# A gated linear attention and its feed-forward layer in one kernel: keys and queries turned in token pairs, and a new order of steps behind the 60th

## The chip, the cores and the metric

The kernel runs on one core of a Trainium2 chip. A core has five engines that run side by side and keep their own order: TensorE (matmuls; in the profile PE, its weight loads PEld), VectorE (DVE), ScalarE (ACT), GpSimd (POOL) and SyncE (SP, which here issues every DMA). They meet through semaphores alone. The metric is the time of one execution in microseconds of device time.

## The reference

For each of 4 batches and 8 heads, over 768 tokens with 48 channels, a state of 48 x 48 decays channel by channel and takes in one token's key and value; each token's query reads it. The result, 3072 tokens by 384, goes through two matmuls (384 x 2048 and 2048 x 384) with a gate between them.

```python
for t in range(S):
    state = alpha[:, :, t, :, None] * state + np.einsum('bhd,bhe->bhde', k[:, :, t], v[:, :, t])
    y[:, :, t] = np.einsum('bhd,bhde->bhe', q[:, :, t], state)
...
h = x @ w_in
relu6 = np.clip(h + 3.0, 0.0, 6.0)
g = h * relu6 / 6.0
return (g @ w_out).astype(np.float32)
```

## The kernel before

**Attention.** The 3072 tokens are 24 chunks of 128 (6 to a batch, `j` from 0 to 23); a chunk holds its 8 heads as 4 pairs (`NP`), each pair in 128 rows (two heads of 48 channels, padded to 64), with 128 tokens along the free dimension. So alpha, keys and queries have to be turned from token rows to channel rows. For chunks below `FIRST` = 6 TensorE does it (`transposed`, steps `ta`, `tk`, `tq`, L282) from the `rings` tiles into PSUM. From chunk 6 on the DMAs of `load_akq` lay 32-token blocks out in `quads` (two per name, `j % 2`), and a DVE transpose of 32 x 32 blocks (`by_blocks`, L286) finishes it: its source has four blocks `v` side by side, token number is 4u + v, and so it writes every fourth float of the target, 16 bytes apart.

With alpha turned in the tile `aX` (129 columns a pair, the first always 0; step `ca`), two DVE scans run over it: `decay` (step `r`, L309) backwards, giving R, products of alpha from a token to the chunk's end, and its reciprocal at the first column into `ini`; `growth` (step `p`, L320) forwards, giving P, growing products that start from that reciprocal. `scaled` (steps `k` and `q`, L332) multiplies keys by R and queries by P. TensorE then makes the scores of two half chunks (`sc`, L346), DVE masks them (`m`, L356), ScalarE lays the queries beside them (`qa`, L366), and `attend` (`ya`, `yb`, L456) multiplies scores and queries with values and state. For the state the keys go back to token rows: `kb` on TensorE below chunk 8, from there on by a DVE transpose (`kt`, L391), a write to DRAM (`kw`, L396) and a read back (`kr`, L404). `update` (`u`, L430) multiplies keys and values, `next_state` (`sm`, L440) adds on DVE, `decayed_state` (`st`, L409) multiplies on POOL, `place_state` (`sv`, L419) copies on ScalarE. The scores, updates and attends are matmuls of 64 rows or 32 to 64 columns; every other matmul of the kernel fills 128 x 128.

**Feed-forward.** Two chunks make a group `g` (0 to 11). `keep_x` (`cy`) puts a chunk's result in the group's `xT`. Groups 0 and 1 use plain matmuls (`fa`, `fb`, `f`: L490, L479); group 0 also the plain second matmul (`b`, L517). From group 2 on the first matmul is done by 20 products of sums of blocks (`M`, L603), for which DVE makes sums of x (`xc`, L540 to L544); ScalarE keeps partial products (`n`, L609), DVE makes outputs of them (`o`), ScalarE and DVE gate them (`e`, L495, and `h`, L499). From group 1 on the second matmul is done by 7 products of half blocks (`P`, L706) with sums on DVE (`s`, L650 and L667), and `K`, `G`, `O` keep, add and store them. The weights come in 16 slices as 64-bit floats (`w`, L162 and L166) and are rounded to 32 bits by ScalarE, DVE and POOL (`d1` to `d4`, L186 to L217).

**Order.** Nothing is scheduled by a planner at build time: the string given to `run` at the end of the kernel lists 1798 steps, name and indices joined by dots (`M.5.14` is product 14 of group 5; `sc.13.3.2` is the scores of chunk 13 in PSUM banks 3 and 2), and each engine, SyncE with its DMAs too, gets its instructions in that order. `z` is a matmul that keeps TensorE running in the first 25 us.

Of the kernel before, what the change touches and what calls it, by code (L numbers as in the profile page):

```python
# [17 lines left out]
def kernel(  # L18
# [208 lines left out]
    Ps = consts.tile([C, NP * W], FP, tag="P", name="P")  # L227
# [46 lines left out]
    def transposed(name, j, i=None):  # L274
        if j >= FIRST:
            t = (K_t if name == "k" else Q_t)[j] = (Ks if name == "k" else Qs)[j % 2]
            by_blocks(t, name, j)
            return
        t = bank("t" + name, j, i)
        src = ring[name, j % NR]  # L280
        for p in range(NP):
            nc.tensor.transpose(  # L282
                t[:, p], src[:, 2 * p : 2 * p + 2].rearrange("s h d -> s (h d)"), ident)

    def by_blocks(to, name, j):
        nc.vector.transpose(out=to.rearrange("r p (u v) -> r p v u", v=V),  # L286
                            in_=quads[name, j % NQ][:, :, :, 0:BLK])

# [15 lines left out]
    def decay(j):  # L304

        n = NP * W
        ax, ic = aX[j % 2], ini[j % 2]
# [5 lines left out]
        nc.vector.reciprocal(out=ic.rearrange("r (p w) -> r p w", w=W)[:, :, 0:1],  # L313
                             in_=R_t[j][:, :, 0:1])

    def growth(j):

        n = NP * W
        P_t[j] = Ps
        nc.vector.tensor_tensor_scan(  # L320
            out=P_t[j], data0=aX[j % 2][:, 0:n], data1=ini[j % 2], initial=0.0,
            op0=ALU.mult, op1=ALU.add)

    def scaled(name, j):

        if j < FIRST:
# [5 lines left out]
        nc.vector.tensor_tensor(out=t, in0=src, in1=by, op=ALU.mult)  # L332
# [424 lines left out]
    with tc.manual_schedule():  # L757
# [15 lines left out]
               q.4 st.4 d1.9 fr.1.1.0 fg.1.1 sv.4.0 f.1.0.2 ca.5 sc.4.1.0 u.4.1.0 fg.0.6 r.5 d1.4
               f.1.7.0 r.6 f.1.3.3 d4.8 d2.4 w.10 tk.5.3 d4.9 w.11 dx.4 fr.1.7.1 sm.4.0 d3.4 w.12
               d2.10 qa.4.0 fg.1.7 fr.1.3.1 m.4 lq.5 d1.10 f.1.6.0 d3.10 d1.12 d4.4 fr.1.0.0 f.1.2.1
               p.5 fg.1.3 d2.12 k.5 fg.1.0 d3.12 d4.10 fr.1.6.1 sm.4.1 tq.5.1 sv.4.1 lk.6 w.13
               fr.1.2.0 d1.11 f.1.4.2 d2.11 d4.12 fg.1.6 q.5 d3.11 p.6 d2.13 la.7 fr.1.4.1 fg.1.4
               f.1.5.0 lv.5.0 qa.4.1 fg.1.2 kb.5.3 fr.1.5.1 w.15 d4.11 d2.15 ca.7 ya.4.1 qa.5.1 tk.6
# [162 lines left out]
```

## Time and profile before

| what | before |
|---|---|
| median of 3 runs | 533.5 us (532.84 to 533.6) |
| the profiled execution's own time | 533.63 us |
| its span, first to last instruction | 531.8 us |
| TensorE matmuls busy | 524.3 us, 99%, clock 1.00 throughout |
| VectorE busy | 475.6 us, 89% |
| ScalarE busy | 261.4 us, 49% |
| DMA, share of 16 engines' span | 42.2% |

The profile is of one execution. A matmul's duration covers its way through the array, so that consecutive ones overlap; the distance from start to start, or from the start of a row of equal matmuls to the next row's start, tells the pace. A group's line gives line number, engine, operation, tiles and shapes, how many, busy time in us, mean ns of one, and the idle time of the engine just before them with what ended it. Line numbers are those of the kernel before.

### The profile page before, as it was taken

How to read it: one execution, taken by the hardware profiler on the slowest of the kernel's cores; microseconds unless marked ns; L12 is line 12 of the kernel's file. 1: busy time of each engine (PE TensorE's matmuls, PEld its weight loads, DVE VectorE, ACT ScalarE, POOL GpSimd, SP SyncE). 2: the span in 40 equal slices, each digit the busy share in tenths (PEclk: the TensorE clock that was granted, in tenths of full speed). 3: DMA queues.
4: the chain of work that ended last, by engine and by line, in shares of the span. 5: the costliest groups of instructions: out<-in, count | busy, mean ns of one | idle time of the engine just before them, and what ended most of it. 6: DMA issues, size and time to landing. Idle time of an engine off the chain costs nothing.

```text
span 531.8 us, 15076 instructions
## 1 busy us (share of the span) xinstructions
PE 524.3 (99%) x6290; PEld 494.0 (93%) x6290; DVE 475.6 (89%) x839; ACT 261.4 (49%) x513; POOL 50.3 (9%) x71
## 2 busy tenths in 40 slices
PE   8999999999999999999999999999999999999997
PEld 5798886789999999999999999999999999999997
DVE  7999999999999999999999999998999999486471
ACT  4888875212664453542673554544454454443330
POOL 5333353100000100000000000000000000000000
PEclk9999999999999999999999999999999999999999
DMA  9999867005363253453463553443531532010000
GB/s 177 246 241 251 247 153 177 2 2 133 74 150 84 64 118 77 115 123 89 95 156 85 120 136 91 96 107 69 145 78 20 129 98 48 1 33 7 9 17 30
DMA packets 124100, 54.40 MB, mean 102 GB/s; under 512 B 83328, under 2 KB 116864, under 8 KB 124032
## 3 DMA queue, kind: packets, MB, share of 16 engines
q1 hardware_dynamic: 124032, 53.44, 42.2%
q8 instruction: 49, 0.80, 0.7%
q14 instruction: 19, 0.16, 0.1%
HBM read 44.50 MB, written 8.91 MB: 100 GB/s over the span
## 4 chain that ended last, share of the span: by engine, by line
PE 85%; DVE 7%; ACT 4%; DMA 1%; issue 1%; SPq 1%; POOL 0%; DVEq 0%; ACTq 0%
PE m_ps L706 36%; PE m_ps L603 31%; PE m_ps L479 4%; PE m_ps L517 4%; PE t_ps L456 4%; PE t_ps L346 2%; PE t_ps L430 2%; DMA rings<-in_q_dram 1%; DVE A L356 1%; ACT A L366 1%; DVE g_sb L540 1%; ACT r L495 1%; ACT raw L186 1%; DVE g_sb L499 1%; SPq L251 1%
## 5 line engine op out<-in xcount | busy, mean ns | idle before, releaser
L706 PE MATMUL m_ps<-w,g_sb 128*128 128x192 f32 x704 | 121.7, 326 | 0.0
L609 ACT COPY g_sb<-m_ps 128x512 f32<-128x512 f32 x110 | 63.5, 584 | 104.2 <-PE m_ps L603 86.4
L706 PEld LDWEIGHTS m_ps<-w,g_sb 128*128 128x128 f32 x704 | 113.7, 190 | 0.6 <-DVE g_sb L667 0.3
L706 PE MATMUL m_ps<-rings,g_sb 128*128 128x192 f32 x528 | 91.7, 327 | 0.2 <-DVE g_sb L650 0.2
L706 PEld LDWEIGHTS m_ps<-rings,g_sb 128*128 128x128 f32 x528 | 85.3, 190 | 0.6 <-DVE g_sb L650 0.5
L603 PE MATMUL m_ps<-xc,w 128*128 128x128 f32 x640 | 83.5, 277 | 0.0
L603 PEld LDWEIGHTS m_ps<-xc,w 128*128 128x128 f32 x640 | 77.9, 192 | 1.1
L495 ACT ACTIVATE r<-g_sb,half 128x512 f32<-128x512 f32 x80 | 57.0, 722 | 29.8 <-DVE g_sb L499 11.9
L499 DVE SCALAR_TENSOR_TENSOR g_sb<-r,g_sb 128x512 f32<-128x512 f32 x80 | 53.5, 682 | 8.7 <-ACT r L495 8.4
L603 PE MATMUL m_ps<-xT,raw 128*128 128x128 f32 x400 | 52.8, 277 | 0.0
L603 PEld LDWEIGHTS m_ps<-xT,raw 128*128 128x128 f32 x400 | 48.8, 192 | 0.5 <-ACT g_sb L609 0.2
L409 POOL TENSOR_TENSOR st<-sm,R 128x192 f32<-128x192 f32 x20 | 12.6, 630 | 358.2 <-DVE sm L440 300.5
L650 DVE TENSOR_TENSOR g_sb<-g_sb 128x512 f32<-128x512 f32 (+1 forms) x55 | 42.1, 792 | 3.7 <-PE m_ps L706 3.5
L603 PE MATMUL m_ps<-xT,w 128*128 128x128 f32 x320 | 42.0, 277 | 0.0
L603 PEld LDWEIGHTS m_ps<-xT,w 128*128 128x128 f32 x320 | 39.0, 192 | 0.4
L366 ACT COPY A<-q 48x256 f32<-48x256 f32 x88 | 35.4, 403 | 7.3 <-DVE q L332 6.1
L356 DVE TENSOR_TENSOR A<-t_ps,mask 64x256 f32<-64x256 f32 x96 | 36.2, 416 | 1.2 <-PE t_ps L346 0.8
L479 PE MATMUL m_ps<-xT,w 128*128 128x256 f32 x144 | 33.3, 384 | 0.5 <-POOL w L217 0.3
L603 PE MATMUL m_ps<-xc,raw 128*128 128x128 f32 x240 | 32.1, 277 | 0.1
L479 PEld LDWEIGHTS m_ps<-xT,w 128*128 128x128 f32 x144 | 26.5, 190 | 5.3 <-POOL w L217 0.9
L540 DVE TENSOR_TENSOR g_sb<-g_sb 128x512 f32<-128x512 f32 x40 | 27.2, 682 | 4.6 <-ACT g_sb L609 4.6
L309 DVE TENSOR_TENSOR_SCAN R<-t,ones 128x516 f32<-128x516 f32 x24 | 29.6, 1233 | 1.6 <-ACT t L300 1.6
(105 smaller groups left out, 726.9 us busy)
## 6 DMA issues: line engine op xcount, KB each, us to landing
raw<-in_moe_w_out_dram SPq DMA_DIRECT2D x8, 768.0 KB, 5.5
raw<-in_moe_w_in_dram SPq DMA_DIRECT2D x6, 768.0 KB, 7.3
v<-in_v_dram SPq DMA_DIRECT2D x48, 96.0 KB, 3.1
out_dram<-oh SPq DMA_DIRECT2D x44, 96.0 KB, 1.8
far<-kq SPq DMA_DIRECT2D x64, 64.0 KB, 2.2
kb<-far SPq DMA_DIRECT2D x64, 64.0 KB, 2.0
aq<-in_alpha_dram SPq DMA_DIRECT2D x36, 96.0 KB, 2.5
kq<-in_k_dram SPq DMA_DIRECT2D x36, 96.0 KB, 2.5
```

The source lines that it names most:

```text
L309: nc.vector.tensor_tensor_scan(out=reverse(R, n - 1, n), data0=reverse(ax, n, n), data1=reverse(ones, n, n), initial=0.0, op0=ALU.mult, op ...
L356: nc.vector.tensor_tensor(out=to[:, a], in0=sc[a][half], in1=mask[half, half].unsqueeze(1).to_broadcast([HB, NP, HB]), op=ALU.mult)
L366: nc.scalar.copy(out=to[:, a], in_=Q_t[j][64 * a : 64 * a + D, :, half])
L456: nc.tensor.matmul(y_of(j, (i + 1) // 2, p)[:, HB * b : HB * b + HB], vb[:, p, e : e + 32], A_t[j][:, b, 2 * p + a], start=(b == 0 and i = ...
L479: nc.tensor.matmul(h[:, f], w1[:, kk, o : o + C], xT_t[g][:, kk], start=(kk == 0), stop=(kk == KT - 1))
L495: nc.scalar.activation(out=to, in_=h, func=AF.Relu, bias=half, scale=1.0 / 6.0)
L499: nc.vector.scalar_tensor_tensor(out=to, in0=r, scalar=1.0, in1=h, op0=ALU.min, op1=ALU.mult)
L540: eng.tensor_tensor(out=out, in0=in0, in1=in1, op=ALU.add if s1 > 0 else ALU.subtract)
L603: nc.tensor.matmul(acc[g][i][:, f * C : (f + 1) * C], spots[w][:, f * C : (f + 1) * C], x_of(g, x), start=(first and f == 0), stop=last, s ...
L609: nc.scalar.copy(out=slots[z], in_=acc[g][i])
L650: nc.vector.tensor_tensor(out=out, in0=in0, in1=in1, op=ALU.subtract)
L706: nc.tensor.matmul(to[g], a, rhs[:, f], start=(first and f == 0), stop=(last and f == HF - 1), skip_group_check=True)
```

## The change

Keys and queries of chunks 6 to 23 are turned by `turned` (L291 of the new kernel) instead of `by_blocks`: the target is a new tile per name (`kt`, `qt`) with the four blocks `v` split in two pairs (w, b), so that tokens 4u + 2w and 4u + 2w + 1 stand next to each other and the next write is 8 bytes on. `scaled` reads pairs from that tile in token order (`in_pairs`) and writes the dense K and Q tiles, which the transposes filled before. P no longer has a tile: below chunk 6 it stands in `qt`, from there on it is scanned over alpha's own tile `aX`, whose first columns a memset on POOL clears again after the queries are scaled. `ini` is one tile instead of two.

The first 60 steps of the order are the same. All steps behind them stand in another order, and PSUM banks are assigned anew; how often each step occurs is unchanged. In the extract of the diff the order is cut to the first lines behind the 60th step and to the places round `M.5.14` (both orders), `u.12`, `lk.17` and `la.18` (the new one).

```diff
@@ -102,14 +102,13 @@
 
 
 
-    aX, ini = [], []
+    aX = []
     for r in range(2):
         t = consts.tile([C, NP * W + 1], FP, tag=f"ax{r}")
         nc.vector.memset(t, 0.0)
         aX.append(t)
-        t = consts.tile([C, NP * W], FP, tag=f"ini{r}")
-        nc.vector.memset(t, 0.0)
-        ini.append(t)
+    ini = consts.tile([C, NP * W], FP, tag="ini")
+    nc.vector.memset(ini, 0.0)
     ones = consts.tile([C, NP * W + 1], FP, tag="ones")
     nc.vector.memset(ones, 0.0)
     nc.vector.memset(ones[:, 1:].rearrange("r (p w) -> r p w", w=W)[:, :, W - 1 : W], 1.0)
@@ -224,7 +223,10 @@
     Rs, Qs, Ks, kbs = (
         [consts.tile([C, *shape], FP, tag=f"{name}{r}", name=f"{name}{r}") for r in range(2)]
         for name, shape in (("R", (NP * W,)), ("q", (NP, C)), ("k", (NP, C)), ("kb", (NP, C))))
-    Ps = consts.tile([C, NP * W], FP, tag="P", name="P")
+    places = {name: consts.tile([C, NP * W], FP, tag=f"{name}t", name=f"{name}t")
+              for name in "kq"}
+    turns = {name: t[:, 0 : NP * C].rearrange("r (w p n) -> r w p n", w=2, p=NP)
+             for name, t in places.items()}
 
     def bank(name, j, i):
         ps_t[name, j] = banks[i].rearrange("r (p n) -> r p n", p=NP)
@@ -273,8 +275,7 @@
 
     def transposed(name, j, i=None):
         if j >= FIRST:
-            t = (K_t if name == "k" else Q_t)[j] = (Ks if name == "k" else Qs)[j % 2]
-            by_blocks(t, name, j)
+            turned(name, name, j)
             return
         t = bank("t" + name, j, i)
         src = ring[name, j % NR]
@@ -286,6 +287,17 @@
         nc.vector.transpose(out=to.rearrange("r p (u v) -> r p v u", v=V),
                             in_=quads[name, j % NQ][:, :, :, 0:BLK])
 
+    def turned(to, name, j):
+        nc.vector.transpose(
+            out=turns[to].rearrange("r w p (u b) -> r p w b u", b=V // 2),
+            in_=quads[name, j % NQ].rearrange("r p (w b) d -> r p w b d", w=2)[..., 0:BLK])
+
+    def in_pairs(to):
+        return turns[to].rearrange("r w p (u b) -> r p u w b", b=V // 2)
+
+    def pairs(x):
+        return x.rearrange("r p (u w b) -> r p u w b", w=2, b=V // 2)
+
     def reverse(t, first, n):
 
         one = t[:, first : first + 1]
@@ -304,33 +316,35 @@
     def decay(j):
 
         n = NP * W
-        ax, ic = aX[j % 2], ini[j % 2]
+        ax = aX[j % 2]
         R = Rs[j % 2]
         nc.vector.tensor_tensor_scan(
             out=reverse(R, n - 1, n), data0=reverse(ax, n, n), data1=reverse(ones, n, n),
             initial=0.0, op0=ALU.mult, op1=ALU.add)
         R_t[j] = R.rearrange("r (p w) -> r p w", w=W)
-        nc.vector.reciprocal(out=ic.rearrange("r (p w) -> r p w", w=W)[:, :, 0:1],
+        nc.vector.reciprocal(out=ini.rearrange("r (p w) -> r p w", w=W)[:, :, 0:1],
                              in_=R_t[j][:, :, 0:1])
 
     def growth(j):
 
         n = NP * W
-        P_t[j] = Ps
-        nc.vector.tensor_tensor_scan(
-            out=P_t[j], data0=aX[j % 2][:, 0:n], data1=ini[j % 2], initial=0.0,
-            op0=ALU.mult, op1=ALU.add)
+        P_t[j] = places["q"] if j < FIRST else aX[j % 2]
+        to = P_t[j][:, 0:n]
+        nc.vector.tensor_tensor_scan(out=to, data0=aX[j % 2][:, 0:n], data1=ini, initial=0.0,
+                                     op0=ALU.mult, op1=ALU.add)
 
     def scaled(name, j):
 
+        t = (K_t if name == "k" else Q_t)[j] = (Ks if name == "k" else Qs)[j % 2]
+        by = R_t[j][:, :, 1:W] if name == "k" else without_first(P_t.pop(j))
         if j < FIRST:
-            src = ps_t.pop(("t" + name, j))
-            t = (Ks if name == "k" else Qs)[j % 2]
-        else:
-            src = t = (K_t if name == "k" else Q_t)[j]
-        by = R_t[j][:, :, 1:W] if name == "k" else without_first(P_t.pop(j))
-        nc.vector.tensor_tensor(out=t, in0=src, in1=by, op=ALU.mult)
-        (K_t if name == "k" else Q_t)[j] = t
+            nc.vector.tensor_tensor(out=t, in0=ps_t.pop(("t" + name, j)), in1=by, op=ALU.mult)
+            return
+        nc.vector.tensor_tensor(
+            out=pairs(t), in0=in_pairs(name), in1=pairs(by), op=ALU.mult)
+        if name == "q":
+            first = aX[j % 2][:, 0 : NP * W].rearrange("r (p w) -> r p w", w=W)[:, :, 0:1]
+            nc.gpsimd.memset(first, 0.0)
 
 
 
@@ -759,153 +773,153 @@
                la.2 z.0.2 ca.0 r.0 z.0.2 lk.0 z.0.8 q.1 d1.0 p.0 lq.0 dx.0 ta.2.0 z.0.2 lv.0.0 d2.0
                tk.0.1 z.0.2 k.0 lk.1 w.1 tq.0.2 ca.2 kb.0.1 z.0.2 w.2 q.0 ck.0 r.2 qa.0.1 lq.2
                sc.0.0.2 z.0.2 z.0.2 la.3 qa.1.0 z.0.3 qa.1.1 m.0 p.2 lk.2 u.0.1.3 tk.1.0 lv.1.1
-               z.0.2 d2.1 sv.0.0 sm.0.0 sm.0.1 d1.1 dx.1 k.1 z.0.2 z.0.1 kb.1.3 la.4 z.0.3 sc.1.0.2
-               ya.0.1 d3.1 ck.1 tq.2.3 d3.0 sv.0.1 m.1 w.3 lq.3 st.1 q.2 yb.0 d2.2 ta.3.0 tk.2.2
-               cy.0 d1.2 d4.0 fa.0.1 k.2 d3.2 dx.2 d4.1 lk.3 sc.2.1.2 u.1.1.2 m.2 ca.3 d4.2 fa.1.2
-               sm.1.0 sv.1.0 w.5 lk.4 sm.1.1 w.6 r.3 sv.1.1 ta.4.0 p.3 ya.1.1 yb.1 cy.1 d2.3 ca.4
-               d3.3 d1.3 lv.2.2 fa.2.0 fb.2 tq.3.0 q.3 lv.3.0 st.2 tk.3.1 k.3 kb.2.2 d4.3 w.7 sv.2.0
-               fb.0 kb.3.0 qa.2.1 d2.5 fr.0.2.0 d1.5 r.4 qa.3.1 fb.1 d2.6 tk.4.3 d3.5 ck.3 fg.0.2
-               f.0.3.3 lq.4 k.4 d4.5 ck.2 d1.6 sc.3.0.2 d3.6 qa.3.0 u.2.3.1 u.3.0.2 w.8 fr.0.3.1
-               fr.0.1.0 qa.2.0 sm.2.0 sm.2.1 sv.2.1 la.5 d4.6 fg.0.3 lk.5 d2.7 d1.7 m.3 st.3 sm.3.0
-               d3.7 qa.0.0 f.0.5.0 fr.0.5.1 fg.0.1 p.4 la.6 sv.3.1 f.0.6.3 ya.2.0 yb.2 sv.3.0
...
-               xc.5.2 M.4.17 h.4.4 lv.13.2 h.4.2 e.4.5.0 n.5.0.14 o.4.7.0 e.4.6.1 u.12.3.0 sc.12.3.0
...
-               M.5.17 G.4.1.2 e.5.4.0 o.5.3.0 cy.12 M.5.13 P.4.6 n.5.13.15 h.5.4 o.5.7.1 M.5.14
...
+               z.0.2 w.3 d2.1 d1.1 sm.0.0 k.1 sv.0.1 dx.1 la.4 kb.1.1 z.0.1 ck.1 sm.0.1 sv.0.0
+               tq.2.3 d3.0 d1.2 sc.1.2.1 d4.0 d3.1 lk.3 st.1 z.0.3 dx.2 q.2 m.1 d2.2 z.0.2 tk.2.3
+               ta.3.0 k.2 ca.3 d3.2 u.1.2.1 sv.1.0 r.3 lq.3 sm.1.0 sm.1.1 ya.0.3 yb.0 cy.0 ta.4.0
+               d4.1 fa.0.1 sv.1.1 ca.4 fa.1.2 sc.2.2.1 p.3 d2.3 d4.2 d3.3 ya.1.0 yb.1 w.5 d1.3 m.2
+               fa.2.0 tk.3.3 lv.3.0 d4.3 k.3 w.6 cy.1 lk.4 st.2 fb.2 kb.2.2 kb.3.1 r.4 lv.2.2 d2.5
+               d1.5 fr.0.2.0 fb.1 ck.2 tq.3.0 qa.2.0 d3.5 tk.4.3 d1.6 k.4 q.3 f.0.3.3 ck.3 sv.2.0
+               d2.6 sc.3.2.1 u.2.0.1 u.3.2.3 qa.3.1 fr.0.3.1 d4.5 w.7 fg.0.2 lq.4 d3.6 f.0.5.0
+               sm.2.0 d2.7 w.8 fg.0.3 d1.7 sv.2.1 kb.4.0 d4.6 ck.4 sm.2.1 st.3 d2.8 la.5 d3.7 sv.3.0
+               qa.3.0 sm.3.0 w.9 f.0.6.3 qa.2.1 lk.5 d4.7 sv.3.1 tq.4.0 fb.0 m.3 sm.3.1 fr.0.1.0
...
+               u.12.3.1 u.13.2.0 h.4.7 qa.13.0 ca.14 s.4.1.12 sc.13.2.1 sc.12.3.0 n.5.2.15 M.5.3
+               s.4.2.9 M.5.4 s.4.3.10 n.5.7.8 r.14 xc.5.2 P.4.2 G.4.0.3 lq.15 sm.12.0 xc.5.8 s.4.4
...
+               o.5.3.1 n.5.13.15 M.5.14 xc.6.3 e.5.3.0 o.5.2.0 o.5.2.1 xc.6.10 lv.15.1 st.14 e.5.2.1
...
+               O.4.3 ca.17 P.5.3.3 s.5.3.15 o.6.0.0 lk.17 sv.14.1 M.6.5 tk.17 st.15 K.5.2 M.6.9
+               tq.16 sm.15.0 sm.15.1 kw.16 lq.18 o.6.1.0 qa.14.0 m.14 sv.15.1 n.6.5.11 O.4.2 r.17
...
+               M.6.18.1 h.6.0 ya.14.1 n.6.18.10 la.18 p.17 ya.15.2 ca.18 n.6.10.15 G.5.1.1 yb.14
...
```

More of the change, by code (lines that the diff above doesn't have):

```diff
@@ L773 @@
[L773 to L778, printed above, removed]
@@ new lines @@
+               lv.12.1 e.3.0.1 M.3.10 s.2.4 s.2.5 e.3.1.0 h.3.1 ca.11 M.3.18.2 n.3.18.15 kw.9 sm.8.0
+               P.2.5 M.3.19 m.8 n.3.10.14 G.2.2.0 h.3.0 M.3.11 P.2.4 kr.9 qa.9.1 r.10 tq.10 sv.8.0
+               la.13 p.10 sm.8.1 M.3.6.3 o.3.6.0 O.2.0 n.3.11.8 tk.10 o.3.5.0 M.3.12 lk.11 O.2.2
+               sc.9.1.2 u.9.0.2 qa.9.0 qa.8.1 k.10 n.3.12.10 st.9 M.3.13 sv.8.1 M.3.15.2 qa.6.0
+               M.3.16 q.10 sv.9.0 m.9 o.3.3.0 sm.9.0 G.2.1.2 sv.9.1 ya.8.3 ya.9.0 yb.8 yb.9
+               n.3.13.10 lv.11.0 o.3.7.0 o.3.4.0 M.3.14 e.3.5.0 o.3.3.1 o.3.2.0 P.2.6 cy.9 cy.8
@@ new lines @@
+               qa.22.1 h.9.6 xc.10.6 xc.10.8 xc.10.10 G.8.3.1 sm.21.1 kt.23 o.9.7.1 M.10.0.0
+               n.10.0.8 e.9.5.0 s.9.0.13 st.22 O.8.1 e.9.7.1 h.9.5 h.9.7 P.9.0.1 s.9.1.12 K.9.0.3
+               xc.10.2 M.10.1 P.9.1 xc.10.0 kw.23 xc.10.7 s.9.4 s.9.2.10 O.8.3 n.10.1.9 M.10.2 tq.23
+               G.9.0.0 M.10.7.2 n.10.2.14 P.9.3.3 s.9.3.13 s.9.5 kr.23 kw.22 M.10.3 M.10.4 n.10.7.11
+               p.23 lv.22.1 n.10.4.15 M.10.8 P.9.2 xc.10.9 K.9.1 o.10.0.0 M.10.9 q.23 P.9.4 kr.22
+               o.10.1.0 lv.23.2 K.9.2 M.10.10 e.10.0.1 u.22.2.0 u.23.3 sc.23.3.0 sc.22.2.1
@@ new lines @@
+               M.11.15.1 M.11.11 n.11.18.14 n.11.11.12 M.11.16 M.11.19 M.11.12 o.11.5.0 O.10.2
+               o.11.4.0 o.11.7.0 P.10.4 n.11.12.11 e.11.4.1 M.11.13 h.11.4 o.11.6.0 G.10.1.1
+               n.11.13.14 M.11.17 M.11.6.3 o.11.3.0 M.11.14 e.11.5.0 h.11.5 o.11.6.1 P.10.6 o.11.3.1
+               e.11.6.1 o.11.7.1 o.11.2.0 h.11.6 P.11.0.1 G.10.3.0 s.11.0.11 e.11.7.1 h.11.7
+               s.11.1.8 K.11.0.0 O.10.3 P.11.3.2 s.11.2.14 o.11.2.1 e.11.3.1 s.11.3.9 h.11.3 s.11.4
+               P.11.2 e.11.2.0 h.11.2 K.11.1 P.11.1 G.11.0.2 K.11.2 s.11.5 P.11.4 G.11.1.0 P.11.5
@@ L912 @@
+               O.11.1 O.11.0 O.10.1 G.11.2.1 P.11.6 O.11.2 G.11.3.2 O.11.3""")
 _INS = ['q', 'k', 'v', 'alpha', 'moe_w_in', 'moe_w_out']
```

243 lines of the change are left out of this document (113 added, 130 removed).

## The prediction

> **What bounds the kernel now.** I read the page's busy shares first, then a table by stage, then the chain of waits, and last TensorE's own waits and its order of instructions in time.
>
> ```profile
> span 531.8 us, 15076 instructions
> PE 524.3 (99%) x6290; PEld 494.0 (93%) x6290; DVE 475.6 (89%) x839; ACT 261.4 (49%) x513; POOL 50.3 (9%) x71
> ```
>
> ```profile
> 100.00:200.00 100.00, 99.83 (x1205) 92.95 (x1204) 97.38 (x176) 42.84 (x89) 3.50 (x6) 1.00 0.36 84
> 200.00:300.00 100.00, 100.00 (x1294) 97.98 (x1293) 98.13 (x176) 47.01 (x101) 2.87 (x5) 1.00 0.46 109
> 300.00:430.00 130.00, 129.82 (x1743) 127.55 (x1742) 124.33 (x223) 62.57 (x132) 3.96 (x6) 1.00 0.42 96
> 460.00:532.00 72.00, 68.95 (x612) 68.44 (x610) 40.17 (x74) 24.45 (x49) 0.00 (x0) 1.00 0.06 18
> ```
>
> The columns of the second fence are the stretch, its length, then the busy time of PE, weight loads, DVE, ACT and POOL, the granted clock, the DMA share and GB/s. Two engines are full at once. TensorE is busy throughout at clock 1.00, and from 100 to 430 us VectorE is busy for 97.38 + 98.13 + 124.33 = 319.8 of 330 us, so it has only 10.2 us to spare there, 4.5 of them before 300 us. After 460 us it has 31.8 us to spare. ScalarE is half idle, and nothing in the middle is bound by DMA.
>
> The chain of waits shows TensorE's pace.
>
> ```profile
> 159.42 2.68 PE m_ps L603 x24
> 162.09 2.60 PE m_ps L706 x16
> 164.70 1.78 PE m_ps L603 x16
> 508.15 20.82 PE m_ps L706 x128
> ```
>
> An L603 matmul takes 2.68/24 = 112 ns and an L706 one 2.60/16 = 163 ns when nothing disturbs them. The last 128 run at 163 ns without a break, so the end is a pure sum of TensorE work; what is saved earlier on TensorE shows whole at the end, and what DVE loses counts only where TensorE then waits. TensorE's waits that the profile sees are few:
>
> ```profile
> PE t_ps L374 <- DVE k L332: 0.8, 1, 0.8
> PE t_ps L282 <- DMA rings<-in_alpha_dram: 0.6, 1, 0.6
> PE t_ps L456 <- DVE s L440: 0.5, 1, 0.5
> PE m_ps L479 <- POOL w L217: 0.3, 1, 0.3
> PE m_ps L479 <- DVE g_sb L499: 0.2, 1, 0.2
> PE m_ps L706 <- DVE g_sb L650: 0.2, 1, 0.2
> ```
>
> All but the last lie before 80 us. So the waits offer about 2 us; the rest has to come from a loss that the busy row hides. TensorE's order in time shows it:
>
> ```profile
> 183.43 1.99 PE L456 MATMUL t_ps<-A,v 128*32 128x64 f32 x128
> 185.36 1.16 PE L603 MATMUL m_ps<-xc,w 128*128 128x128 f32 x8
> ```
>
> ```profile
> 21.86 0.65 PE L456 MATMUL t_ps<-A,v 128*32 128x64 f32 x32
> 22.45 0.66 PE L282 MATMUL t_ps<-ident,rings 128*128 128x128 f32 x4
> ```
>
> ```profile
> 233.25 0.83 PE L603 MATMUL m_ps<-xT,raw 128*128 128x128 f32 x6
> 234.01 0.57 PE L430 MATMUL t_ps<-v,kb 64*48 64x48 f32 x32
> 234.41 0.66 PE L346 MATMUL t_ps<-q,k 48*64 48x64 f32 x32
> 235.00 2.05 PE L603 MATMUL m_ps<-xc,w 128*128 128x128 f32 x16
> 236.89 1.30 PE L706 MATMUL m_ps<-w,g_sb 128*128 128x192 f32 x7
> ```
>
> Columns are start, duration, then the instructions. The attention's small matmuls (L346 scores, L430 state update, L456 attend) sit between full 128x128 ones, and each trip to them and back costs three gaps. Going back: 128 attends in one run take 185.36 - 183.43 = 1.93 us to the next full matmul, 32 alone take 22.45 - 21.86 = 0.59; with f for 32 and e for the exit, 4f + e = 1.93 and f + e = 0.59, so f = 0.45 and e = 0.14. After the return: 16 L603 matmuls take 236.89 - 235.00 = 1.89 us against 1.78 undisturbed, 0.11 more. Going in: the six L603 from 233.25 should end after 6 x 0.112 = 0.67 at 233.92, the first small one starts at 234.01, 0.09 later. Together 0.34 us a trip. Between L430 and L346 nothing of the kind is seen: 32 take 0.40 us, entry behind them.
>
> **The change, part by part.** *The order of steps.* Every TensorE step occurs as often as before, so its work is the same. I counted in both orders, as built, how often a run of small matmuls returns to full ones: 39 times before, 29 after, because scores and updates of two chunks now stand together, and so do attends. Ten trips fewer are 10 x 0.34 = 3.4 us less on the engine that sets the end.
>
> Of the waits, the 0.8 us before the second chunk's key transposes (L374) shortens by about one state addition, since the new order puts k.1 ahead of sm.0.1 on DVE; the 0.5 us before L456 falls, since two weight products and the scores of chunk 2 now stand between the update and the attend that needed it. That is some 0.3 + 0.5 = 0.8 us. The moved weight slices and the waits behind them (0.3 + 0.2) I take as unchanged: the queue of DMA issues has slice 3 one place earlier, slices 5 to 8 where they were, and TensorE uses slices 3, 5 and 6 within 1.5 us of where it did. Late next is whatever the denser groups put behind them: masks for two chunks now stand close on DVE, and both chunks' attends wait for the later one.
>
> *Keys and queries in token pairs.* Rows for both engines:
>
> ```profile
> L286 DVE STREAM_TRANSPOSE k<-kq x18: 1085/1111/1184, 81.6 to 426.0; 128x512 f32<-128x512 f32 x18
> L286 DVE STREAM_TRANSPOSE q<-qq x18: 1052/1118/1153, 89.0 to 445.4; 128x512 f32<-128x512 f32 x18
> L391 DVE STREAM_TRANSPOSE kq<-k x16: 669/704/719, 136.7 to 440.7; 128x512 f32<-128x512 f32 x16
> L332 DVE TENSOR_TENSOR k<-k,R 128x512 f32<-128x512 f32 x18 | 12.3, 685 | 0.1
> L332 DVE TENSOR_TENSOR q<-q,P 128x512 f32<-128x512 f32 x18 | 12.2, 681 | 0.2
> L257 POOL MEMSET kq<- 32x64 f32 x4 | 0.6, 145 | 0.2
> L409 POOL TENSOR_TENSOR st<-sm,R 128x192 f32<-128x192 f32 x20 | 12.6, 630 | 358.2 <-DVE sm L440 300.5 <-ACT v L419 43.7 <-DMA raw<-in_moe_w_in_dram 11.9
> ```
>
> The 36 transposes of chunks 6 to 23 now write neighbours 8 bytes apart, where L286 wrote 16 bytes apart (1.11 us) and L391 writes them 4 apart (0.70). The price lies between: a gain of 0 to 0.41 us each. Taken linearly in the step, 0.70 + 0.41 x 4/12 = 0.84, so 0.28 us each, 36 x 0.28 = 10 us of DVE over the whole run. The 36 multiplies read pairs from two places instead of a dense tile: 0 to +0.41 us by the same two rows; I take 0, as they still write densely like the L332 rows, and keep 0.41 for the range. So DVE's load changes by -15 to +15 us, and I take -10. None of this is on the path by itself: TensorE is the engine that ends last, and a lighter DVE is cover for the new order.
>
> The Trainium skill, SBUF — State Buffer, section "Door 1: The DMA port swizzle", says that SBUF works in 16-byte lines and that two hits in a line are enough for full bandwidth. By that rule a step of 8 bytes would cost what L391 does and the multiplies would cost nothing more: an estimate of 36 x 0.41 = 15 us of relief in place of 10. L286 against L391 agrees with it at the two ends; no row here has pairs.
>
> The new order spends that relief. DVE's other prices, and how its instructions overlap:
>
> ```profile
> L309 DVE TENSOR_TENSOR_SCAN R<-t,ones 128x516 f32<-128x516 f32 x24 | 29.6, 1233 | 1.6 <-ACT t L300 1.6
> L320 DVE TENSOR_TENSOR_SCAN P<-t 128x516 f32<-128x516 f32 x24 | 30.4, 1267 | 0.2
> L540 DVE TENSOR_TENSOR xc<-xT,xc 128x128 f32<-128x128 f32 x40 | 11.1, 282 | 0.3
> ```
>
> ```profile
> 205.52 0.67 DVE L332 TENSOR_TENSOR k<-k,R 128x512 f32<-128x512 f32 x1
> 206.09 1.29 DVE L650 TENSOR_TENSOR g_sb<-g_sb 128x512 f32<-128x512 f32 x2
> ```
>
> Counted in the two orders, DVE has 11 steps more ahead of the product M.5.14 than before: two ca, two tk and one tq (5 x 1.11), r (1.23 and 0.2 for its reciprocal), p (1.27), k (0.69), kt (0.70) and two xc (2 x 0.28), 10.2 us by duration. An instruction overlaps the next by 0.1 (0.57 from start to start for 0.67), 12 x 0.1, so 9.0 us. 21 of the pair transposes lie ahead of that point. At 0.28 they give 5.9 back, and the remaining 3.1 us fit into the 4.5 us that DVE has to spare up to 300 us.
>
> *Smaller edits.* P written over alpha's tile leaves the scan what it was; its first columns are cleared by 18 POOL memsets (0.15 us each by L257). The scan r of the chunk after next waits for that, and behind the memset on POOL stands only the state's decay st (0.63 us, idle 358 us before it); both are hidden. One `ini` tile puts r of a chunk behind p of the chunk before, both on DVE in that order. One memset less on DVE at the start is hidden: the transposes that follow wait for alpha's landing (0.6 us, above). Loads keep their number; they land in 2.0 to 6.3 us:
>
> ```profile
> DMA to landing us min/median/max: 2.0/2.5/6.3
> ```
>
> *Sum,* against the profiled execution's own 533.6 us (span 531.8 and 1.8 around it; the median of the runs is 533.5): 533.6 - 3.4 - 0.8 = 529.4, and I add 0.4 for new waits of the size of the last row of TensorE's waits, two of them: 529.8 us.
>
> **Rivals.** *DVE late in the middle (slower).* If pairs cost as much as L286 and gain nothing, DVE stands 9.0 - 4.5 = 4.5 us behind at M.5.14 and TensorE waits for sums and gates there: 529.8 + 4.5 = 534.3. If the multiplies also cost up to 0.41 more, 19 of them by that point add up to 7.8 us: 542. It turns slower than now from 1.07 + 3.7 = 4.8 us of lateness on, that is when the 40 pair steps up to there cost 0.3 us more than before together. For it speaks that DVE is 98% busy from 200 to 300 us; against it, that step size is what separates L286 from L391.
>
> *Loads late, nothing gained.* Several fetches now stand nearer to their use in the order (lk.17 and la.18 less than 1 us of TensorE work ahead of it). SyncE issues in order behind writes and stores; with four loads 0.9 us late beyond DVE's cover the gain is gone: 533.5. Against it: in the profile before no DVE idle time in the middle ends on a DMA, though some loads stood as near.
>
> *The waits go altogether (faster still).* If DVE has 15 us of relief and the remaining 2 us of early waits go too: 528.0.
>
> **How the numbers follow.** My case, 528.3 to 531.4, has 0.61; faster than that 0.06; partly eaten by loads or DVE, 531.4 to 534.6, 0.14, half of it within 0.2% of 533.5 (532.4 to 534.6, about what a measurement here can tell from no change); slower 0.19. So faster 0.74, same 0.07, slower 0.19. The range 527.6 to 534.6 leaves out the slower case and little else, 2 in 10.
>
> **What would show it.** After: the pair transposes' line at 0.70 to 0.85 us and the multiplies' at 0.68; TensorE's small matmuls in groups of 64 to 128 with 29 returns; TensorE's work ending near 525 us; no DVE idle time that ends on a DMA. The forecast is wrong if the multiplies pass 0.9 us, if L603 or L706 in 200 to 300 us wait for DVE g_sb by more than 1 us, or if weight slices make L479 wait longer than the 0.3 us now.

## The result, and the profile after

The changed kernel takes 530.89 us (median of 6 runs, 530.5 to 531.17) against 533.2 us for the kernel before on the same chip (532.53 to 533.79): a ratio of 0.9955, with a 95% interval of 0.9945 to 0.9965. That is 2.3 us less by the medians; the forecast was 3.7 us less than 533.5. The profiled execution took 530.91 us, with a span of 529.1 instead of 531.8, 2.7 us less.

From the page of the changed kernel, the span and the busy time of each engine:

```profile
span 529.1 us, 15082 instructions
PE 520.6 (98%) x6290; PEld 494.8 (94%) x6290; DVE 462.0 (87%) x838; ACT 259.6 (49%) x513; POOL 55.3 (10%) x89
```

VectorE is 13.6 us lighter (475.6 to 462.0). The table by stage, with the same columns as in the prediction (stretch, length, PE, weight loads, DVE, ACT, POOL, clock, DMA share, GB/s):

```profile
100.00:200.00 100.00, 99.61 (x1297) 94.01 (x1296) 97.77 (x181) 44.82 (x96) 3.82 (x10) 1.00 0.37 87
200.00:300.00 100.00, 99.75 (x1380) 98.44 (x1380) 97.40 (x180) 46.44 (x100) 5.82 (x11) 1.00 0.47 110
300.00:430.00 130.00, 130.00 (x1644) 128.72 (x1643) 116.86 (x220) 62.50 (x132) 3.79 (x11) 1.00 0.36 86
460.00:532.00 72.00, 66.26 (x593) 65.75 (x591) 38.64 (x70) 24.17 (x49) 0.00 (x0) 0.98 0.05 16
```

From 200 to 300 us TensorE issues 1380 matmuls where it issued 1294. That is no faster pace: 128 more of the attends, of 14 ns each, fall into this stretch. VectorE is as full as it was up to 300 us (97.77 and 97.40, before 97.38 and 98.13); its relief is seen only behind that (116.86 of 130, before 124.33). TensorE's waits:

```profile
PE t_ps L283 <- DMA rings<-in_q_dram: 1.5, 1, 1.5
PE m_ps L548 <- POOL ident masks.py:199: 1.5, 1, 1.5
PE t_ps L388 <- DVE k L341: 1.0, 1, 1.0
PE t_ps L283 <- DMA rings<-in_alpha_dram: 0.8, 1, 0.8
PE t_ps L470 <- DVE s L454: 0.4, 1, 0.4
PE m_ps L617 <- ACT g_sb L623: 0.3, 1, 0.3
PE t_ps L470 <- DVE k L341: 0.2, 1, 0.2
```

The first, third and fourth, 3.3 us together, lie between 18 and 28 us. Early waits did not shrink, they grew, in this execution at least: in the profiles of the two later groups below, the same kernel's wait for in_q is 0.28 us and nothing. Where the time went I took from TensorE's order in time: for each matmul the distance to the next one's start, less the undisturbed distance for its shape (112 ns for a 128x128 one, 163 for a 128x192 one and so on). The undisturbed sum is 506.6 us in both kernels; what is left over, by stage, is TensorE's loss (a return counts where its row of small matmuls starts; the profiled execution before is 0.4 us above its median, so the sum is 2.7 us where the medians give 2.3):

| stage, us | loss before | loss after | change | returns to full matmuls, before and after |
|---|---|---|---|---|
| 0 to 30 | 6.77 | 8.63 | +1.9 | 6, 4 |
| 30 to 100 | 3.80 | 1.42 | -2.4 | 5, 4 |
| 100 to 200 | 3.33 | 3.51 | +0.2 | 8, 7 |
| 200 to 310 | 2.92 | 2.15 | -0.8 | 9, 6 |
| behind 310 | 3.88 | 2.30 | -1.6 | 11, 8 |
| sum | 20.7 | 18.0 | -2.7 | 39, 29 |

### The profile page after: what moved, and what is told of

Read it like the earlier page. It is cut to its first block, busy times and chain, and to the rows that moved or that the text cites. A ratio compares the mean times of both kernels' runs of the same rounds, so it can differ in the third digit from the quotient of the medians.

```text
span 529.1 us, 15082 instructions
## 1 busy us (share of the span) xinstructions
PE 520.6 (98%) x6290; PEld 494.8 (94%) x6290; DVE 462.0 (87%) x838; ACT 259.6 (49%) x513; POOL 55.3 (10%) x89
## 4 chain that ended last, share of the span: by engine, by line
PE 90%; DVE 4%; SPq 2%; DMA 2%; ACT 1%; issue 1%; POOL 0%; DVEq 0%; POOLq 0%; ACTq 0%
PE m_ps L720 36%; PE m_ps L617 31%; PE m_ps L493 6%; PE m_ps L531 4%; PE t_ps L470 4%; PE t_ps L360 2%; PE m_ps L504 2%; PE m_ps L548 2%; PE t_ps L444 1%; PE t_ps L283 1%; DMA rings<-in_alpha_dram 1%; DVE g_sb L554 1%; SPq L253 1%; PE t_ps L388 1%; SPq L410 0%
## 5 line engine op out<-in xcount | busy, mean ns | idle before, releaser
L617 PE MATMUL m_ps<-xc,w 128*128 128x128 f32 x640 | 82.1, 276 | 0.3 <-ACT g_sb L623 0.3
L617 PEld LDWEIGHTS m_ps<-xT,w 128*128 128x128 f32 x320 | 39.0, 192 | 0.4
L370 DVE TENSOR_TENSOR A<-t_ps,mask 64x256 f32<-64x256 f32 x96 | 36.1, 415 | 0.4
L423 POOL TENSOR_TENSOR st<-sm,R 128x192 f32<-128x192 f32 x20 | 14.7, 737 | 157.2 <-DVE sm L454 157.1
L554 DVE TENSOR_TENSOR g_sb<-m_ps,g_sb 128x512 f32<-128x512 f32 x30 | 20.5, 683 | 11.4 <-PE m_ps L617 7.0
```

The source lines that it names most:

```text
L370: nc.vector.tensor_tensor(out=to[:, a], in0=sc[a][half], in1=mask[half, half].unsqueeze(1).to_broadcast([HB, NP, HB]), op=ALU.mult)
L554: eng.tensor_tensor(out=out, in0=in0, in1=in1, op=ALU.add if s1 > 0 else ALU.subtract)
L617: nc.tensor.matmul(acc[g][i][:, f * C : (f + 1) * C], spots[w][:, f * C : (f + 1) * C], x_of(g, x), start=(first and f == 0), stop=last, s ...
```

## The experiments

Three medians of the changed kernel stand for comparison: 530.89 above, and one on the chip of each of two later groups, 531.27 and 530.80.

### The pair transposes without the new order

The steps stay in the order of before; three of them move, by up to 33 of the 1798 places, because tiles are shared now (tk.22 behind k.21, p.5 ahead of r.6, p.17 ahead of r.18). 39 returns to full matmuls, as before.

> The token pairs alone, with the order of before (three steps moved by a few places, since the single ini and kt tiles want p.5 and p.17 ahead of the next chunk's r and tk.22 behind k.21); 39 trips of small matmuls, as before. Theory A (TensorE sets the end and the trips are the gain): DVE loses some 13 us of work, TensorE keeps its 39 trips and only its few waits on DVE shrink, so 532.2 to 533.4 us against 533.2 of before. Theory B (DVE's relief itself is the gain): most of the 2.3 us, 530.9 to 531.5 us.

532.56 us (532.2 to 533.24), ratio 0.9987 [0.9978, 0.9996]: the lighter VectorE by itself is worth about 0.7 us, in the range of theory A. Its stage from 200 to 300 us:

```profile
200.00:300.00 100.00, 100.00 (x1294) 98.25 (x1293) 95.31 (x179) 48.37 (x105) 4.43 (x12) 1.00 0.45 107
```

VectorE falls from 98.13 to 95.31, and TensorE, at 1294 matmuls as before, gets no more done in this stretch. Relief of an engine that isn't waited for is worth almost nothing.

### The new order without the relief

The pair transposes write 16 bytes apart again, into the same tiles, and the multiplies read them densely; the order stays new.

```diff
-            out=turns[to].rearrange("r w p (u b) -> r p w b u", b=V // 2),
-            in_=quads[name, j % NQ].rearrange("r p (w b) d -> r p w b d", w=2)[..., 0:BLK])
+            out=dense(to).rearrange("r p (u v) -> r p v u", v=V),
+            in_=quads[name, j % NQ][:, :, :, 0:BLK])
...
-            out=pairs(t), in0=in_pairs(name), in1=pairs(by), op=ALU.mult)
+            out=t, in0=dense(name), in1=by, op=ALU.mult)
```

> The changed kernel with its new order and tiles, but keys and queries written 16 bytes apart again and read densely: 36 transposes at 1.11 us where the changed kernel has 0.70. Theory A (the new order spends DVE's relief): DVE is 36 x 0.41 = 14.8 us fuller, 9.0 us of work stand ahead of M.5.14 where 4.5 us are to spare, TensorE waits for DVE between 200 and 310 us, 533.5 to 537 us. Theory B (DVE was never near the path; the order alone is the change): 530.5 to 531.3 us.

538.59 us, ratio 1.0105 [1.0089, 1.012], slower than either kernel and 7.7 us above the changed one: what theory A said, and 1.6 us beyond its range. The transposes' group, the table by stage, and those of TensorE's waits that are new or longer than in the changed kernel (this kernel's lines stand three lower from there on):

```profile
L291 DVE STREAM_TRANSPOSE kt<-kq 128x512 f32<-128x512 f32 x18 | 20.2, 1123 | 0.0
```

```profile
100.00:200.00 100.00, 97.97 (x1280) 91.91 (x1280) 98.56 (x178) 43.99 (x94) 3.30 (x9) 1.00 0.35 83
200.00:310.00 110.00, 107.51 (x1425) 104.57 (x1424) 106.88 (x189) 47.72 (x103) 6.33 (x12) 1.00 0.46 108
```

```profile
PE t_ps L473 <- DVE s L457: 1.0, 1, 1.0
PE m_ps L620 <- DVE g_sb L559: 0.8, 1, 0.8
PE m_ps L620 <- DVE xc L557: 0.7, 1, 0.7
PE m_ps L723 <- DVE g_sb L561: 0.7, 1, 0.7
PE t_ps L473 <- DVE A L373: 0.5, 1, 0.5
```

At 1.12 us a transpose VectorE is 98.6% busy and TensorE waits for its sums, gates and states. Against the changed kernel the step M.2.14 starts 1.3 us later, M.4.14 2.4, M.5.14 5.1, M.6.14 6.5, M.9.14 7.4; behind that the lag stays. So the new order and the pairs are worth something only together: order alone 5.3 us slower than before, pairs alone 0.7 faster, both 2.3 faster.

### Twelve trips put back

In twelve places of the changed kernel one full product is put into the middle of a group of small matmuls; 41 returns instead of 29, nothing else moves.

```diff
-               ... u.12.3.1 u.13.2.0 h.4.7 qa.13.0 ca.14 s.4.1.12 sc.13.2.1 sc.12.3.0 ...
+               ... u.12.3.1 u.13.2.0 h.4.7 qa.13.0 ca.14 s.4.1.12 M.5.2 sc.13.2.1 sc.12.3.0 ...
```

> The changed kernel with 12 groups of small matmuls split by one full product each (41 returns from small to full matmuls instead of 29), nothing else. Theory A (each trip costs TensorE 0.34 us): 530.9 + 12 x 0.34 = 535.0 us, between 534.3 and 535.6. Theory B (the gaps are hidden by other waits, or a trip in mid-group is cheaper): under 532.5 us.

535.03 us, ratio 1.0039 [1.0025, 1.0053]: 4.1 us above the changed kernel's 530.89, 0.345 us a trip (by the spans, 533.1 and 529.1, 0.33; by the ratios 0.37). Theory A holds. The figure is a mean: by the same sum of distances TensorE lost 0.2 us more for the one trip between 100 and 200 us, 0.9 for the four up to 310 us and 3.0 for the seven behind, so a trip doesn't cost the same everywhere.

### One start-up wait at a time

Three edits, each against one of the three early waits, with the changed kernel itself beside them.

```diff
-  z.0.2 w.3 d2.1 d1.1 sm.0.0 k.1 sv.0.1 dx.1 la.4 kb.1.1 ...
+  z.0.2 la.4 w.3 d2.1 d1.1 sm.0.0 k.1 sv.0.1 dx.1 kb.1.1 ...
```

```diff
-  tq.2.3 d3.0 d1.2 sc.1.2.1 d4.0 d3.1 lk.3 st.1 z.0.3 dx.2 ...
+  d3.0 d1.2 sc.1.2.1 z.0.3 tq.2.3 d4.0 d3.1 lk.3 st.1 dx.2 ...
```

```diff
-  ... m.0 p.2 lk.2 ... k.1 sv.0.1 ...
+  ... m.0 lk.2 ... k.1 p.2 sv.0.1 ...
```

> The changed kernel as it stands, timed beside the three edits of its start-up on the same chip. Both theories: 530.9 us, as before (530.5 to 531.2).

> The load la.4 is issued ahead of the weight slice w.3 again. In the changed kernel its transposes wait 0.80 us for in_alpha at 27.9 us. Theory S1 (what TensorE waits for in the first 30 us sets the end): the wait goes, 0.8 us less, 530.1 us. Theory S2 (VectorE and the weight slices behind the start-up set when the 60th step can run, TensorE's early waits are refilled by later ones): within 0.3 us of the changed kernel, 530.6 to 531.2 us, and the wait turns up behind it, on w.3 or on the next VectorE result.

> The transposes tq.2, which wait 1.46 us for in_q at 21.3 us in the changed kernel, stand behind sc.1 and the filler z.0.3, as before the change. Theory S1: up to 1.3 us less, 529.6 us (the scores of chunk 1 and the filler, 1.3 us of work, are done inside the wait). Theory S2: within 0.3 us of the changed kernel, 530.6 to 531.2 us: tq.2 is then there no later, but the wait reappears on VectorE's side, since q.2 follows k.1 and w on VectorE's queue.

> VectorE's scan p.2 stands behind the multiply k.1, for which the transposes kb.1 wait 1.02 us at 18.9 us in the changed kernel. p.2 takes 1.3 us of VectorE and is wanted only by q.2. Theory S1: kb.1 starts 1.0 us earlier, 529.9 to 530.2 us. Theory S2: within 0.3 us of the changed kernel, 530.6 to 531.2 us: kb.1 starts earlier and a later start-up wait grows by as much.

| kernel | median, us | ratio to before, interval |
|---|---|---|
| changed kernel, same chip | 531.27 | 0.9959 [0.9946, 0.9972] |
| la.4 ahead of w.3 | 530.68 | 0.9949 [0.9937, 0.9961] |
| tq.2 behind sc.1 and z.0.3 | 531.17 | 0.9966 [0.9953, 0.9979] |
| p.2 behind k.1 | 531.31 | 0.9963 [0.9951, 0.9974] |

Theory S1 falls for the second and third. For the first it is not decided: four of its five times (530.35 to 530.86 us) lie below all five of the changed kernel on that chip (531.02 to 531.37), 0.6 us less by the medians, where S1 said 0.8 and S2 at most 0.3. But the intervals of the ratios overlap, and no later kernel with this edit repeats the gain. The waits show what the other two met. First the kernel with tq.2 moved, then the one with p.2 moved:

```profile
PE t_ps L360 <- ACT kb L392: 1.4, 1, 1.4
PE t_ps L283 <- DMA rings<-in_alpha_dram: 0.4, 1, 0.4
```

```profile
PE t_ps L283 <- DMA rings<-in_q_dram: 2.3, 1, 2.3
PE t_ps L388 <- DVE k L341: 0.3, 1, 0.3
PE t_ps L283 <- DMA rings<-in_alpha_dram: 0.3, 1, 0.3
```

Where tq.2 no longer waits for in_q, sc.1 waits 1.4 us for ScalarE's copy of kb.1; where kb.1 waits 0.7 us less, tq.2 waits 0.9 us more for in_q. Both then wait for in_alpha ahead of ta.4, which starts at 27.93 and 27.83 us, as in the changed kernel, where the transposes ta.4 and the first full weight product (fa.0) are these rows of TensorE's order in time:

```profile
27.91 0.63 PE L283 MATMUL t_ps<-ident,rings 128*128 128x128 f32 x4 [0.80 <-DMA rings<-in_alpha_dram]
28.37 2.84 PE L504 MATMUL m_ps<-xT,w 128*128 128x128 f32 x24
```

In all three fa.0 starts right behind ta.4, at 28.3 to 28.4 us. So in these profiles the landing of la.4 sets that point, and what is won ahead of it goes into the wait for it. Only the first edit moves the landing. Its wait is gone and ta.4 starts at 27.50 us, but fa.0 not before 28.27; in this execution the granted clock (third from the right) was low just ahead of it, where the three others have 1.00:

```profile
22.00:24.00 2.00, 2.00 (x25) 1.24 (x18) 2.00 (x4) 1.97 (x3) 1.97 (x3) 0.70 1.04 177
24.00:26.00 2.00, 2.00 (x19) 1.67 (x20) 1.81 (x5) 0.81 (x3) 0.83 (x1) 0.50 0.90 324
```

So this profile can't show what the edit is worth. Its three executions at a mean clock of 1.00 have spans of 528.6 to 528.9 us, the changed kernel's two on that chip 529.5 and 529.6, and its ten such executions on all chips 528.7 to 529.6.

### VectorE beside GpSimd, and all edits together

VectorE works almost without a gap from 16 to 30 us, and two of its instructions there are stretched beside GpSimd's additions (L216). VectorE's and GpSimd's order in time in the changed kernel:

```profile
19.77 0.69 DVE L204 TENSOR_SCALAR w<-w 128x768 uint32<-128x768 uint32 x1
...
21.09 2.03 DVE L204 TENSOR_SCALAR w<-w 128x768 uint32<-128x768 uint32 x1
...
29.16 1.90 DVE L333 TENSOR_TENSOR_SCAN qt<-t,ini 128x516 f32<-128x516 f32 x1
```

```profile
20.70 1.86 POOL L216 TENSOR_TENSOR w<-w,raw 128x768 int32<-128x768 int32 x1 [13.14 <-DVE w L204]
...
27.32 2.65 POOL L216 TENSOR_TENSOR w<-w,raw 128x768 int32<-128x768 int32 x1 [2.22 <-DVE w L204]
```

One kernel leaves the additions of slices 0 to 2 out. Another makes the three edits above at once and puts ScalarE's copy ck.1 ahead of its long step dx.1. A third also changes VectorE's order.

```diff
+        if i < 3:
+            return
         dst, lo, hi = slice_of(i)
```

```diff
-  ... d3.0 d1.2 sc.1.2.1 z.0.3 tq.2.3 d4.0 d3.1 lk.3 st.1 dx.2 q.2 m.1 ... k.2 ca.3 d3.2 u.1.2.1 sv.1.0 r.3 lq.3 sm.1.0 sm.1.1 ... p.3 ...
+  ... d3.0 d1.2 sc.1.2.1 z.0.3 tq.2.3 d4.0 m.1 q.2 d3.1 lk.3 st.1 dx.2 ... k.2 ca.3 u.1.2.1 sv.1.0 r.3 lq.3 sm.1.0 sm.1.1 p.3 d3.2 ...
```

> The changed kernel as it stands, on the same chip as the next three. 531.0 us (530.9 and 531.3 before).

> GpSimd's additions of the low bits to weight slices 0 to 2 are left out, so the first three slices of moe_w_in are only the high part. What is told apart: whether VectorE's stretched instructions beside them (2.03 instead of 0.69 us at 21.1 us, 1.90 instead of 1.23 us at 29.2 us in the changed kernel) are caused by the additions, and whether they are what the end hangs on. Both theories: the two take 0.69 and 1.23 us if the additions cause it. Theory V (VectorE's queue sets when TensorE gets going): 1.3 to 2.0 us less than the changed kernel, 529.0 to 529.7 us. Theory L (a loop of several engines and loads does: in_q at 21.3 us and in_alpha at 27.9 us bind as soon as VectorE doesn't): within 0.4 us of the changed kernel, 530.6 to 531.0 us.

> The three start-up edits of the runs before at once (la.4 ahead of w.3, sc.1 and the filler ahead of tq.2, p.2 behind k.1), and ScalarE's copy ck.1 ahead of its 1.9 us step dx.1, for which sc.1 waited 1.4 us in the second of them. Theory V (VectorE sets the start-up, its order of slices unchanged): within 0.4 us of the changed kernel, 530.6 to 531.2 us, and the transposes tk.2 wait for q.2, which stands behind VectorE's stretched 2.03 us instruction. Theory L (one wait hides the next, so that all have to go): 1.0 us less, 529.8 to 530.2 us.

> As the run above, and VectorE's order changed so that it reads PSUM (m.1, q.2, then sm.1) or has no GpSimd addition beside it where it was stretched: d3.1 stands behind m.1 and q.2, and r.3, sm.1 and p.3 ahead of d3.2. Theory V: both stretches go (2.03 to 0.69 us, 1.90 to 1.23 us), q.2 ends about 1.1 us earlier, and the time is 1.0 to 1.5 us below the changed kernel, 529.5 to 530.0 us. Theory L: as the run above within 0.3 us.

| kernel | median, us | ratio to before, interval |
|---|---|---|
| changed kernel, same chip | 530.80 | 0.9955 [0.9943, 0.9968] |
| additions of slices 0 to 2 left out | 530.78 | 0.9957 [0.9944, 0.9970] |
| all three edits, ck.1 ahead of dx.1 | 531.48 | 0.9964 [0.9952, 0.9976] |
| the same, VectorE's order changed | 531.46 | 0.9966 [0.9954, 0.9977] |

Without the additions both instructions have their usual length, in VectorE's order in time of that kernel (its lines stand two lower from there on):

```profile
21.12 0.69 DVE L204 TENSOR_SCALAR w<-w 128x768 uint32<-128x768 uint32 x1
...
28.43 1.22 DVE L335 TENSOR_TENSOR_SCAN qt<-t,ini 128x516 f32<-128x516 f32 x1
```

So the additions cause the stretch, shown. But 2.0 us less on VectorE moved the median by nothing: theory V falls, and the time is the one that theory L gave. (The profiled execution of the kernel without additions was the slowest of its six, 532.75 us, so its times are not compared. In it TensorE came to ta.4 early and waited 2.2 us for in_alpha, as theory L has it.) The next two kernels remove the waits together, and their medians are 0.7 us above that of the changed kernel: against theory L, which promised 1.0 us less for the first, and above theory V's range for it (531.2) too. From their waits, of the kernel with the three edits and then of the one with VectorE's order changed too:

```profile
PE t_ps L283 <- DVE q L341: 2.2, 1, 2.2
PE t_ps L360 <- ACT kb L392: 0.2, 1, 0.2
```

```profile
PE m_ps L504 <- POOL w L216: 1.4, 1, 1.4
PE t_ps L283 <- DVE q L341: 1.1, 1, 1.1
```

In the first, in_q binds no more and kb.1 hardly, and tk.2 waits for q.2, which stands behind the stretched L204, as theory V said; the clock was at 0.50 from 26 to 28 us in this execution too. In the second the stretch went elsewhere (r.3's scan took 2.39 us, a later L207 1.94), so what theory V gave for its going was not put to the test. There, at a clock of 1.00, ta.4 ran at 27.07 us without a wait and fa.0 started at 27.85, 0.5 us earlier than in the changed kernel; the weight slice whose step d3.2 had been put back was then late by 1.4 us. Each engine's start-up order is balanced against the others': of the waits that I removed, all but that for in_alpha came back at a neighbour, and where that one went together with others, the time was no better.

### A late wait

```diff
-  ... ya.8.3 ya.9.0 yb.8 yb.9 ...
+  ... ya.8.3 yb.8 ya.9.0 yb.9 ...
```

> The changed kernel with la.4 ahead of w.3 (530.68 us by itself, beside 531.27 for the changed kernel on that chip) and with the second half of chunk 8's attends ahead of the first half of chunk 9's, which wait 0.36 us for VectorE's state at 183.3 us; the 32 attends put between them take 0.45 us and need only chunk 8. If a late wait shows whole at the end, as the sum of losses has it: the wait goes and the span is 0.4 us below that of the run with la.4 alone (529.1), 528.7 us, time 530.3 us (529.9 to 530.7). If VectorE is late by more than that, the wait moves to the attends behind and the time stays at 530.7 us.

531.07 us, ratio 0.9960 [0.9946, 0.9973]. TensorE's order in time around this place, first of the changed kernel, then of this one:

```profile
182.24 0.65 PE L470 MATMUL t_ps<-A,v 128*32 128x64 f32 x32
183.25 1.55 PE L470 MATMUL t_ps<-A,v 128*32 128x64 f32 x96 [0.36 <-DVE s L454]
184.72 1.16 PE L617 MATMUL m_ps<-xc,w 128*128 128x128 f32 x8
```

```profile
182.44 2.16 PE L470 MATMUL t_ps<-A,v 128*32 128x64 f32 x128
184.65 1.16 PE L617 MATMUL m_ps<-xc,w 128*128 128x128 f32 x8
```

From the first attend to the next full product it is 2.21 us instead of 2.48: the wait is gone, 0.27 us won there. Against the kernel with la.4 alone, whose profile has the same mean clock (0.997), this one is 0.2 us behind out of its start-up (M.2.14 at 147.1 and 146.8 us), 0.1 ahead at M.3.14 and 0.3 behind again at M.5.14 (268.5 and 268.2). It lost the gain in four steps of about 0.1 us each (ahead of M.4.0, M.3.17, M.5.9 and M.5.18), too small for the list of waits; what they are I did not find. The median lies above both cases that were expected (530.3 and 530.7), on another chip than la.4 alone. So this wait doesn't show at the end either. No kernel among these is shown to be faster than the changed one.

## Why the prediction came out as it did

The time was in the range and on the side named as likeliest; the gain was forecast 1.1 us too large by the spans (3.8 against 2.7). By its terms, with the measured 0.345 us for each trip wherever it lies, which is an assumption:

| term | forecast, us | measured or left over, us | from |
|---|---|---|---|
| ten trips fewer | -3.4 | -3.45 | 10 x 0.345 |
| waits of the start-up | -0.8 | +0.5 | up to 100 us the loss changed by -0.52, of which three trips make -1.03 |
| new waits | +0.4 | +0.25 | behind 100 us it changed by -2.17, of which seven trips make -2.4 |
| sum | -3.8 | -2.7 | |

The range held although the start-up went the wrong way by 1.3 us, because it was wide. That the 0.4 us for new waits, a guess, lies near the 0.25 left over is luck.

*Trips: right.* The price worked out from three gaps (0.34) is what twelve trips put back cost in the mean (0.345), and TensorE's loss went down with them.

*Start-up: the step that failed.* The forecast said that the wait before the second chunk's key transposes would shorten by 0.3 us and the one before L456 would fall. The first went from 0.8 to 1.0 us. The second went, but the attends of chunk 0 wait 0.2 us in its place, and two loads that were hidden are not. tq.2 stands ahead of sc.1 and waits 1.46 us for in_q, ta.4 waits 0.80 for in_alpha, since w.3 is fetched ahead of la.4. I had priced two waits from one engine's order and never looked at what stands next to be late on the other three; the prediction even took the fetches as unchanged. The first 30 us got 1.9 us worse, and the next 70 us gave 2.4 back. Of these waits the one for in_alpha is the last ahead of fa.0; those for k.1 and in_q cost nothing by themselves, as they were taken away one at a time at 531.31 and 531.17 us beside 531.27. What the wait for in_alpha costs stays open: 0.6 us by the medians of one chip, and nothing to be seen in three further kernels that have this edit together with others.

*Pairs: right in kind, the other bound in size.* I took 0.28 us a transpose, between 0 and 0.41. Measured, in the groups of the changed kernel:

```profile
L291 DVE STREAM_TRANSPOSE kt<-kq 128x512 f32<-128x512 f32 x18 | 12.7, 704 | 0.0
L291 DVE STREAM_TRANSPOSE qt<-qq 128x512 f32<-128x512 f32 x18 | 12.6, 699 | 0.0
L343 DVE TENSOR_TENSOR k<-kt,R 128x512 f32<-128x512 f32 x18 | 12.2, 680 | 0.1
L343 DVE TENSOR_TENSOR q<-qt,t 128x512 f32<-128x512 f32 x18 | 12.2, 675 | 0.0
```

0.70 us, the full 0.41, and the multiplies at 0.68 as before. The rule quoted from the Trainium skill (SBUF — State Buffer, "Door 1: The DMA port swizzle") gave 15 us of relief and was right; the linear reading gave 10. By the page VectorE is 13.6 us lighter; 36 x 0.41 = 14.8, and the stretch beside GpSimd took 1.2 more than before (2.0 against 0.8).

*The order spends the relief: right in mechanism, too small in size.* With no relief I forecast VectorE 4.5 us behind at M.5.14, and that at the end. The run without relief was 5.1 behind at that step and 7.4 at the end. The count of steps ahead was good; what failed was to stop it at one point, as the denser groups behind 270 us added 2.3 us.

*Rivals.* The slower one needed pairs that gain nothing; its mechanism is real (1.0105), its condition did not hold. Loads in the middle: VectorE's only idle time that ends on a DMA is 2.7 us before the last outputs, at 524 us. The faster one failed, as the early waits did not go.

## What to carry to other kernels

Price a switch between kinds of matmul from its gaps and count the switches: that term held (0.34 us forecast, 0.33 to 0.37 measured). Relief on a second engine that is just as full is worth little by itself (0.7 us here) and may be the condition for an order that gains, so measure the pair and not the parts. In a start-up where four engines and the loads hand work round, do not add up waits from one engine's view: find the wait that ends last ahead of the next stage, since what is won ahead of it goes into it, and ask of each engine what would hold the stage once that wait is gone. Look at the clock rows before you compare two profiles there.

## What the runs showed of the hardware

A VectorE instruction that begins beside GpSimd's int32 addition seems to stand still until the addition is over: the L204 that begins at 21.09 us ends at 23.12, 0.56 after the addition's end at 22.56, where one alone takes 0.69, and the scan L333 ends 1.09 after the next such end (29.97), where one alone takes 1.22. VectorE's instructions that read PSUM beside an addition kept their length: the four L370 from 23.63 us took 1.52 beside the addition from 23.25 to 25.11, and 1.53 in the kernel without additions. The Trainium skill, SBUF — State Buffer, section "Who interferes with whom", says that whichever of the two issues first holds the shared pair of ports for the whole instruction and the other blocks. These rows agree, and so does the run without the additions.

In some runs TensorE's clock is halved for a few microseconds in the start-up. The table by stage of the changed kernel on the second chip, of the kernel with la.4 and the late wait edited, and of the kernel before (clock third from the right):

```profile
22.00:24.00 2.00, 2.00 (x32) 1.55 (x33) 2.00 (x2) 1.97 (x2) 1.97 (x3) 0.55 0.85 185
24.00:26.00 2.00, 2.00 (x9) 1.43 (x8) 1.61 (x5) 1.36 (x2) 1.58 (x1) 0.60 1.07 338
```

```profile
20.00:22.00 2.00, 0.99 (x7) 0.52 (x5) 1.93 (x4) 2.00 (x3) 0.81 (x1) 0.91 1.00 127
22.00:24.00 2.00, 2.00 (x35) 1.57 (x35) 2.00 (x2) 1.97 (x2) 1.97 (x3) 0.50 0.93 163
24.00:26.00 2.00, 2.00 (x12) 1.53 (x10) 1.75 (x6) 1.32 (x2) 1.57 (x1) 0.73 1.00 325
```

```profile
18.00:20.00 2.00, 1.18 (x7) 0.88 (x6) 1.86 (x5) 1.97 (x3) 0.49 (x1) 1.00 1.36 226
20.00:22.00 2.00, 1.99 (x46) 1.38 (x50) 1.93 (x4) 1.98 (x4) 0.03 (x1) 1.00 1.03 124
```

In the second fence (0.09 + 0.50 + 0.27) x 2 us = 1.7 us of clock are missing; at half speed that is a stretch of 3.4 us, and the first fence gives the same. Ahead of it TensorE was busy for about 2 of 4 us (0.98 and 0.99 in the second kernel); before the change it was busy for 3.2 of them and none of 45 runs shows a mean clock below 0.999. Being half busy doesn't bring it by itself: the changed kernel's first profile has 1.62 of the 4 us from 18 to 22 and a clock of 1.00 behind them. Of 16 runs of the changed kernel six show 0.997. Their spans average 529.3 us against 529.2 for the others, so here it costs little, probably because the slow stretch lies ahead of the wait for in_alpha. With la.4 fetched earlier it is 529.1 and 529.3 in two such runs and 528.6 to 528.9 in the other three; the kernel with tq.2 moved has 530.4 in three such runs and 529.2 in the other three. The Trainium skill, TensorE: Matmul & The Clock Gate, section "Part 1: The HAM clock gate", says that a monitor with a free-running window of 3.4 us halves the clock after an idle window. The length agrees, and that only some runs of one kernel are hit speaks for a window that runs freely; but behind 12 us TensorE was not idle for 3.4 us in any profiled execution (the longest gap is 2.33 us), only half busy.
